# Hedgehog attention beside a gated feed-forward: the last two heads' rows in spare rows of the output projection

## The chip, the cores and the metric

The kernel runs on one core of a Trainium2 chip. The core has five engines that run side by side and wait for each other through semaphores: TensorE (PE in the profile, with PEld for its weight loads), VectorE (DVE), ScalarE (ACT), GpSimd (POOL) and SyncE (SP), which here only issues DMA transfers. Each engine takes its instructions in order. The metric is the time of one execution on the device in microseconds; the kernel before has a median of 693.31 us in three runs (691.02 to 696.13).

## The reference

All tensors are float32. The sequence has S = 2048 tokens, the model width is D = 640, there are H = 32 heads of Dh = 20, and the feed-forward width is F = 1536.

```python
xn = layernorm(x)
q, k, v = split(xn @ wqkv)                       # 32 heads of 20
phi(u) = concat(softmax(u @ w_phi), softmax(-(u @ w_phi)))    # 40 features for each head
kv = sum over tokens of phi(k)^T v               # 40 x 20 for each head
z  = sum over tokens of phi(k)
o  = (phi(q) kv) / (phi(q) z + 1e-6)
s  = o @ wo
g  = silu(gelu(xn @ w1 + b1) @ w2 + b2)
return x + s * g
```

## The kernel before, in words

**Precision.** Nearly all products run in float32r on operands split into a high part and a remainder: three matmuls (PASSES, L296: high x high, high x low, low x high) stand for one float32 product.

**Phase 1** (L436 to L560) works through sixteen token tiles of 128: layer norm, projections, the two softmaxes, and the sum kv over the tokens. The unnormalized query features of each tile go to DRAM (e_dram).

**Feed-forward** (L834 to L960) consists of twelve units: two halves of the tokens (1024 each) by six groups of 256 hidden columns. A unit has seven products of 128x512 blocks (PARTS, a Strassen-like scheme), gelu, and two calls of `down` (L638), which multiply by w2 for the two 512-token chunks of the half and add to the accumulators y. Beside them the units normalize query tiles: `q_norm` (L689) is a generator whose steps are placed by hand between the products. It multiplies the features by the key sums on POOL (L692), sums heads and takes reciprocals on DVE (L694 to L705), scales on POOL (L346) and stores to phi_dram on SP (L709). The table QN (L819) says which tiles a unit takes; units 1 to 5 and 7 to 10 take tiles 8 to 15 and 0 to 3. Unit 11, the last, takes none.

**Output projection** (L984 to L1001) has four chunks of 512 tokens in the order 2, 3, 0, 1. For each chunk `num_groups` (L760) transposes the normalized query features (`num_t`, L729) and multiplies them by the kv of the heads (`num_m`, L742). The 1280 features stand in eleven tiles: ten of 120 rows (three heads of 40) and one of 80 (heads 30 and 31). Two tiles make one output tile oT[0][j], j = 0 to 4: rows 0 to 59 hold three heads of 20, rows 64 to 123 the next three, and eight rows are spare and zero. Heads 30 and 31 have 40 rows, for which there is a tile of their own, oT[1]: they are put three times below each other, by two matmuls of 64 and 56 columns (L753, L754), as high, high and low copies (the selectors lowsel and midsel), so that one matmul of 120 rows does the three passes. `finish` (L800) makes one block of 128 output columns by 512 tokens: 15 matmuls over the five oT tiles and a sixteenth for the last two heads (L803) with the weights `wol` (L711). DVE multiplies the result by the gate, POOL adds the residual, and SP stores it (L815).

The work on a chunk's products is done one chunk ahead. For the first chunk it runs inside the last call of `down` (L959), in groups of three, and the first `finish` follows. For the others it runs between the blocks of the chunk before, in groups of four: block, transposes, and the products of the group before. Query tiles 4 to 7 are normalized during the first two chunks (`late_q`, L964), since their phi is first loaded for the fourth chunk (L998, in the second chunk after its fourth block).

**Order.** From the first unit on every engine's order is that of the program, written by hand (`manual_schedule`, L832); on PE and SP it is so from the start. SP's order therefore matters: it holds the loads of the residual (`load_res`, L780, two blocks ahead of use), the loads and stores of the query tiles, the phi loads (`load_phi`, L723) and the result stores. The buffers come from pools: 23 slabs, 11 rows, and 13 tiles in the pool of the late stage; an instruction that fills a buffer waits until its last user is done.

Of the kernel before, what the change touches and what calls it, by code (L numbers as in the profile page):

```python
# [8 lines left out]
F32 = mybir.dt.float32  # L9
F32R = mybir.dt.float32r  # L10
# [35 lines left out]
def hedgehog_gated_mlp_kernel(ctx: ExitStack, tc: tile.TileContext, x, xt_in, wqk, bd, wv, wo, w1, b1, w2, b2, out_t):  # L46
# [33 lines left out]
    def row(shape, dt, name):  # L80
        return rows.tile(shape, dt, tag="R", name=name)
# [27 lines left out]
    for h in range(3):  # L109
# [4 lines left out]
    lowsel = const.tile([P, 1], F32, name="lowsel")  # L114
    nc.gpsimd.memset(lowsel[:], -1.0)
    nc.gpsimd.affine_select(out=lowsel[:], in_=lowsel[:], pattern=[[0, 1]],
                            compare_op=OP.is_ge, fill=0.0, base=-80, channel_multiplier=1)
    midsel = const.tile([P, 1], F32, name="midsel")
    nc.gpsimd.memset(midsel[:], -1.0)
    nc.gpsimd.affine_select(out=midsel[:], in_=midsel[:], pattern=[[0, 1]],  # L120
                            compare_op=OP.is_ge, fill=0.0, base=-40, channel_multiplier=1)
    nc.gpsimd.affine_select(out=midsel[:], in_=midsel[:], pattern=[[0, 1]],
                            compare_op=OP.is_ge, fill=0.0, base=79, channel_multiplier=-1)
    const.tile([P, 8], F32, name="align")
    bdk = const.tile([P, 10, 64], F32, name="bdk")
    bdl = const.tile([P, 120], F32, name="bdl")


    def load_x(t):
# [442 lines left out]


    def kv_state(kvr):
        nc.gpsimd.memset(bdk[:, :, 60:], 0.0)
        ps = bankB()
        for g, m in enumerate((P, P, 96)):
            nc.tensor.transpose(ps[:120, g * P:g * P + m], kvr[:m, 120 * g:120 * g + 120], ident[:m, :m])
        s3 = ps[:120, :320].rearrange("p (f r) -> p f r", r=32)
        nc.vector.tensor_tensor(bdk[:120, :, :60].rearrange("p f (h d) -> p f h d", d=20),  # L580
                                s3[:, :, None, :20].to_broadcast([120, 10, 3, 20]),
                                mask[:120, None, :, None].to_broadcast([120, 10, 3, 20]), op=OP.mult)
        for r in range(3):
            nc.vector.tensor_tensor(bdl[:80, 40 * r:40 * r + 40].rearrange("p (h d) -> p h d", d=20),
                                    ps[:80, None, 320:340].to_broadcast([80, 2, 20]),
                                    mask[:80, :2, None].to_broadcast([80, 2, 20]), op=OP.mult)
    def kv_norm(kvr):
        zf = slab(F32, "zrep")[:].rearrange("p a b -> p (a b)")
        for e, n in enumerate((360, 360, 320, 240)):
# [90 lines left out]
        nc.sync.dma_start(xd_dram[:, :, 1, at(p)], tt)  # L680


    def q_load(t):
        e = slab(F32, "eq")
        ef = e[:].rearrange("p a b -> p (a b)")
        nc.sync.dma_start(ef, e_dram[t])
        return ef

    def q_norm(t, ef):  # L689
        ez = slab(F32, "ez")  # L690
        zv = ez[:].rearrange("p a b -> p (a b)")
        nc.gpsimd.tensor_tensor(zv, ef, zf, op=OP.mult)  # L692
# [12 lines left out]
        nc.vector.tensor_tensor(r3, r3, den[:, :, None].to_broadcast([P, 32, 2]), op=OP.mult)  # L705
        yield
        scale_heads(ef, rc)
        yield
        nc.sync.dma_start(phi_dram[t], ef)  # L709

    def load_wol():  # L711
        raw = row([P, D], F32, "raw")
        for r in range(3):
            nc.sync.dma_start(raw[40 * r:40 * r + 40, :], wo[640:680, :])
        wol_h = row([P, D], F32R, "wolh")
        wol = row([P, D], F32R, "wol")
        nc.vector.tensor_copy(wol_h[:120, :], raw[:120, :])
        nc.vector.scalar_tensor_tensor(wol[:120, :], wol_h[:120, :].bitcast(F32), midsel[:120, :], raw[:120, :],
                                       op0=OP.mult, op1=OP.add)
        return wol  # L720


    def load_phi(c):  # L723
        tl = [slab(F32R, "phi", (P, 2 * D)) for _ in range(TPC)]
# [17 lines left out]
    def num_m(j, oT, p, n, ph):  # L742
        po = bankB()
        sl = slice(256 * p, 256 * p + 256)
        if j < 5:
            for e in range(2):
                nc.tensor.matmul(po[64 * e:64 * e + 64, :256], bdk[:n, 2 * j + e, :], ph[:n, e * 256:(e + 1) * 256],  # L747
                                 start=True, stop=True)
            o2 = oT[0][j]
            nc.scalar.activation(o2[:, 0, sl], po[:, :256], AF.Copy)  # L750
            nc.vector.tensor_tensor(o2[:, 1, sl], po[:, :256], o2[:, 0, sl].bitcast(F32), op=OP.subtract)
        else:
            for a, b in ((0, 64), (64, 120)):  # L753
                nc.tensor.matmul(po[a:b, :256], bdl[:n, a:b], ph[:n, :256], start=True, stop=True)  # L754
            o2 = oT[1]
            nc.scalar.activation(o2[:120, 0, sl], po[:120, :256], AF.Copy)
            nc.vector.scalar_tensor_tensor(o2[:120, 1, sl], o2[:120, 0, sl].bitcast(F32), lowsel[:120, :],
                                           po[:120, :256], op0=OP.mult, op1=OP.add)

    def num_groups(phi, oT, size=4):  # L760
        steps = [(j, p) for p in range(2) for j in range(6)]
        before = []
        for k in range(0, 12, size):
            now = [(j, p, *num_t(phi, p, j)) for j, p in steps[k:k + size]]
            for j, p, n, ph in before:
                num_m(j, oT, p, n, ph)
            before = now
            yield
        for j, p, n, ph in before:
            num_m(j, oT, p, n, ph)  # L770
        yield

    def new_oT(home):
# [26 lines left out]
    def finish(c, d, oT, last):  # L800
        ps = bankB()
        steps = [(wo_s[j][:, b, d * P:(d + 1) * P], oT[0][j][:, a, :]) for j in range(5) for a, b in PASSES]
        steps.append((wol[:120, d * P:(d + 1) * P], oT[1][:120, 1, :]))  # L803
        for n, (w, o) in enumerate(steps):
            nc.tensor.matmul(ps[:], w, o, start=n == 0, stop=n == 15)  # L805
        xr, gt = xres.pop((c, d)), gates.pop((c, d))
        for o in range(2):
            sl = slice(o * W2, (o + 1) * W2)
            g = gt[:, sl]
            nc.vector.tensor_tensor(g, ps[:, sl], g, op=OP.mult)  # L810
            (nc.vector if last else nc.gpsimd).tensor_tensor(xr[:, sl], g, xr[:, sl], op=OP.add)
            if last:
                nc.sync.dma_start(out_t[d * P:(d + 1) * P, c * CW + o * W2:c * CW + (o + 1) * W2], xr[:, sl])
        if not last:
            nc.sync.dma_start(out_t[d * P:(d + 1) * P, c * CW:(c + 1) * CW], xr[:])  # L815


    zf, none = None, iter(())
    QN = {1: (8,), 2: (9,), 3: (10,), 4: (11,), 5: (12,), 7: (13, 14), 8: (15, 0), 9: (1, 2), 10: (3,)}  # L819
    units = NH * NG  # L820

    def w2_raw(g):
# [11 lines left out]
    for unit in range(units):  # L834
# [116 lines left out]
        if unit == NG - 1:  # L951
            held = list(ys)
            ys[:] = [None] * KC
    wol = load_wol()
    oT = new_oT(late)
    qe[4] = q_load(4)
    load_res(0)
    load_res(1)
    for _ in down(g, w2g, hs, 1, num_groups(phi, oT, 3)):  # L959
# [2 lines left out]
    gate(1)  # L962

    def late_q():  # L964
        qn = q_norm(4, qe.pop(4))
        next(qn)
        for t in range(4, 8):
            if t < 7:
                qe[t + 1] = q_load(t + 1)
            next(qn)  # L970
            yield
            next(qn)
            yield
            next(qn)
            next(qn)
            yield
            next(qn, None)
            if t < 7:
                qn = q_norm(t + 1, qe.pop(t + 1))
                next(qn)  # L980
            yield

    lq = late_q()
    for ci, c in enumerate(ORDER):  # L984
        nxt = iter(())
        if ci + 1 < NCH:
# [2 lines left out]
        for d in range(KC):  # L989
# [4 lines left out]
            if ci == 0 and d % 2 == 0:  # L994
                next(lq, None)
            next(nxt, None)
            if ci + 2 < NCH and d == (0 if ci == 0 else 3):
                phin = load_phi(ORDER[ci + 2])  # L998
            next(lq, None)
# [5 lines left out]
def _layout(A_x, A_wqkv, A_w_phi, A_wo, B_w1, B_b1, B_w2, B_b2):  # L1005
# [5 lines left out]
    wo = np.zeros((680, D), a["wo"].dtype)  # L1011
    for k in range(10):
        wo[64 * k:64 * k + 60] = a["wo"][60 * k:60 * k + 60]
    wo[640:] = a["wo"][600:]
# [37 lines left out]
```

## Time and profile before

| what | value |
|---|---|
| median of three runs | 693.31 us (691.02 to 696.13) |
| span of the profiled execution, first to last instruction | 688.8 us |
| the profiled execution's own time | not recorded beside its span |
| what the median has above that span | 4.5 us |
| mean granted TensorE clock | 0.996 of full speed |
| unit 11 (544.7 to 581.4) | 36.7 us |
| output projection, four chunks (581.4 to 683.95) | 102.6 us |
| from the last matmul to the end | 4.85 us |

A group in the profile is given by its line, engine and operation, then output and inputs by the program's names, shapes, the number of instructions, the busy time in us and the mean of one in ns, and last the engine's idle time ahead of them with what ended it. Matmuls overlap in the pipeline, so the mean of one is longer than the distance from one start to the next. A row of the timeline has start and length in us, engine, line, and how many instructions of a kind were merged; in brackets stands the wait ahead of the first. A row of the windows has, for each engine, the busy time and the number of instructions in that stretch. SPq rows are transfers as SP issues them.

### The profile page before, as it was taken

What the parts mean: (1) busy time and instruction counts of PE and PEld (TensorE: products, weight loads), DVE (VectorE), ACT (ScalarE), POOL (GpSimd) and SP (SyncE); (2) the same over time, 40 slices, a digit from 0 to 9 for tenths busy, and PEclk for the clock granted to TensorE, in tenths of its full rate; (3) what the DMA queues carried; (4) which work ended last, traced back from release to release, by engine and by line L of the source; (5) the groups of instructions that cost most, each with busy time, mean ns of one, the idle gap of its engine ahead of it and who ended that gap; (6) DMA issues with size and microseconds to landing.
All of it is one profiled execution on the core that took longest, in us unless ns stands there. A gap on an engine that the chain in (4) does not pass through costs nothing.

```text
span 688.8 us, 12182 instructions
## 1 busy us (share of the span) xinstructions
PE 680.1 (99%) x4833; PEld 592.8 (86%) x4833; DVE 453.4 (66%) x730; ACT 251.3 (36%) x398; POOL 376.8 (55%) x336
## 2 busy tenths in 40 slices
PE   8899999999999999999999999999999999999997
PEld 8899999999999998888888888888888887777875
DVE  4688556887667546667978774677977655774232
ACT  3331322332332227343353346632232353425430
POOL 1354344948587455946878853636356640783221
PEclk9999999999999999999999999999999999999999
DMA  9830052824172144328697697276364391886633
GB/s 327 288 104 2 3 149 79 245 68 160 35 212 77 72 145 169 115 69 292 220 328 253 202 429 323 81 272 230 140 218 152 132 391 65 320 292 203 234 92 107
DMA packets 73967, 125.57 MB, mean 182 GB/s; under 512 B 5694, under 2 KB 42686, under 8 KB 73014
## 3 DMA queue, kind: packets, MB, share of 16 engines
q1 hardware_dynamic: 71606, 114.31, 48.8%
q10 hardware_dynamic: 2304, 10.49, 4.3%
q8 instruction: 38, 0.62, 0.4%
q14 instruction: 19, 0.16, 0.1%
HBM read 79.68 MB, written 45.10 MB: 181 GB/s over the span
## 4 chain that ended last, share of the span: by engine, by line
PE 96%; DMA 1%; DVE 1%; issue 1%; POOL 1%; ACT 0%; SPq 0%; POOLq 0%; DVEq 0%
PE pA L307 30%; PE pB L646 24%; PE pB L617 21%; PE pB L805 11%; PE pB L747 3%; PE pA L164 2%; PE pB L736 2%; PE kv L378 2%; DMA folds<-in_wqk_dram 1%; PE pA L293 1%; PE pB L754 1%; PE pB L591 0%; POOL e L328 0%; POOL wv L138 0%; ACT e L333 0%
## 5 line engine op out<-in xcount | busy, mean ns | idle before, releaser
L646 PE MATMUL pB<-hs,w2s 128*128 128x512 f32 x720 | 167.1, 390 | 0.0
L646 PEld LDWEIGHTS pB<-hs,w2s 128*128 128x128 f32 x720 | 134.7, 188 | 29.3 <-PE pB L747 0.8
L617 PE MATMUL pB<-xp,w1s 128*128 128x512 f32 x324 | 81.3, 389 | 0.0
L617 PE MATMUL pB<-xd,w1s 128*128 128x512 f32 x324 | 79.3, 389 | 0.0
L333 ACT ACTIVATE e<-e 128x1280 f32<-128x1280 f32 x32 | 40.7, 1271 | 90.0 <-POOL e L328 90.0
L805 PE MATMUL pB<-oT,wo 128*128 128x512 f32 x300 | 72.9, 395 | 0.0
L655 DVE TENSOR_TENSOR y<-pB,y 128x512 f32<-128x512 f32 x100 | 63.8, 680 | 12.3 <-PE pB L646 12.1
L617 PEld LDWEIGHTS pB<-xd,w1s 128*128 128x128 f32 x324 | 60.8, 188 | 12.6
L617 PEld LDWEIGHTS pB<-xp,w1s 128*128 128x128 f32 x324 | 60.8, 188 | 12.6
L805 PEld LDWEIGHTS pB<-oT,wo 128*128 128x128 f32 x300 | 55.4, 188 | 14.8 <-ACT ph L739 1.2
L346 POOL TENSOR_TENSOR e<-e,rc 128x1280 f32<-128x1280 f32 x16 | 39.0, 2438 | 49.1 <-DVE rc L366 48.8
L346 POOL TENSOR_TENSOR eq<-eq,rc 128x1280 f32<-128x1280 f32 x16 | 37.9, 2370 | 50.2 <-DVE rc L705 50.2
L328 POOL TENSOR_TENSOR e<-nr,e 128x640 f32<-128x640 f32 x32 | 45.5, 1422 | 34.6 <-DVE nr L327 31.7
L307 PE MATMUL pA<-wv,xp 128*128 128x320 f32 x384 | 61.1, 312 | 0.8 <-DVE nr L327 0.4
L307 PE MATMUL pA<-wk,xp 128*128 128x320 f32 x384 | 61.5, 316 | 0.0
L622 ACT ACTIVATE pB<-pB,b1t 128x512 f32<-128x512 f32 x48 | 31.8, 662 | 76.2 <-PE pB L617 26.7
L307 PE MATMUL pA<-wq,xp 128*128 128x320 f32 x384 | 59.0, 309 | 0.0
L307 PEld LDWEIGHTS pA<-wk,xp 128*128 128x128 f32 x384 | 58.3, 193 | 0.2
L307 PEld LDWEIGHTS pA<-wv,xp 128*128 128x128 f32 x384 | 56.9, 188 | 1.7 <-issue 0.7
L307 PEld LDWEIGHTS pA<-wq,xp 128*128 128x128 f32 x384 | 56.9, 188 | 0.1
L692 POOL TENSOR_TENSOR ez<-eq,zrep 128x1280 f32<-128x1280 f32 x16 | 47.3, 2958 | 0.5 <-DMA eq<-e_dram 0.5
L402 POOL TENSOR_TENSOR w1s<-raw,w1s 128x640 fp32r<-128x640 f32 (+1 forms) x18 | 25.7, 1429 | 37.1 <-ACT w1s L401 29.9
(139 smaller groups left out, 1045.2 us busy)
## 6 DMA issues: line engine op xcount, KB each, us to landing
raw<-in_w_dram SPq DMA_DIRECT2D x42, 320.0 KB, 4.4
e_dram<-e ACTq DMA_DIRECT2D x16, 640.0 KB, 4.0
eq<-e_dram SPq DMA_DIRECT2D x16, 640.0 KB, 7.0
phi_dram<-eq SPq DMA_DIRECT2D x16, 640.0 KB, 3.5
phi<-phi_dram SPq DMA_DIRECT2D x16, 640.0 KB, 8.5
xt<-in_x_dram SPq DMA_DIRECT2D x16, 320.0 KB, 4.9
xres<-in_xt_dram SPq DMA_DIRECT2D x20, 256.0 KB, 4.8
out_dram<-xres SPq DMA_DIRECT2D x18, 256.0 KB, 3.0
```

The source lines that it names most:

```text
L307: nc.tensor.matmul(ps[:, hf, :HALF], stat_x(q, o, k, a), ws[k][:, b, hf * HALF:(hf + 1) * HALF], start=n == 0, stop=n == 3 * KC - 1)
L328: nc.gpsimd.tensor_tensor(e5[:, :, :, 1, :], nr[:, :, :, None].to_broadcast([P, 2, 16, DH]), e5[:, :, :, 0, :], op=OP.subtract)
L333: nc.scalar.activation(ef, ef, AF.Exp)
L346: nc.gpsimd.tensor_tensor(e3, e3, rc[:, :, None].to_broadcast([P, 64, DH]), op=OP.mult)
L402: nc.gpsimd.tensor_tensor(sl[:, 1, :n], src, sl[:, 0, :n].bitcast(F32), op=OP.subtract)
L617: nc.tensor.matmul(bank[ch][:], tl[:, a, off + wo_:off + wo_ + P], mov(blk, b), start=new and n == 0, stop=n == len(mms) - 1, skip_group_c ...
L622: nc.scalar.activation(ps, ps, AF.Gelu_apprx_tanh, bias=b1t[:, f:f + 1])
L646: nc.tensor.matmul(ps[:], ws[i][:, b, d * P:(d + 1) * P], hs[o][i][:, a, :], start=i == n == 0, stop=(i, n) == (GF - 1, 2), skip_group_che ...
L655: nc.vector.tensor_tensor(y, ps[:], y, op=OP.add)
L692: nc.gpsimd.tensor_tensor(zv, ef, zf, op=OP.mult)
L747: nc.tensor.matmul(po[64 * e:64 * e + 64, :256], bdk[:n, 2 * j + e, :], ph[:n, e * 256:(e + 1) * 256], start=True, stop=True)
L805: nc.tensor.matmul(ps[:], w, o, start=n == 0, stop=n == 15)
```

## The change

Heads 30 and 31 lose their own sixteenth matmul. Their 40 output rows are shared out to the 40 spare rows of the five oT[0][j] tiles, eight to each. For this the layout of an oT tile changes: every sixteenth row (15, 31, ... 127) is spare, and the rows between hold five-row pieces of three heads; the rows of wo are permuted in the same way on the host (640 rows in place of 680). kv_state builds the block weights bdk in that order, by three multiplications in place of one, and bdl once in place of three times. `num_m` computes the last two heads with one matmul of 40 columns. A new function `spread(j, oT)` copies eight rows of oT[1], high and low part (8 x 4 KB), into the spare rows of oT[0][j], by a transfer from SBUF to SBUF on SP's queue, right after the second half (p = 1) of tile j is done. The products start with j = 5, so that their rows are there first. `load_wol`, lowsel and midsel go.

In the output projection the result stores, and the phi stores of `late_q`, are collected (`put`) and issued by `put_all` after the step of `num_groups` in the same block, and so behind the spread transfers on SP. Query tile 4 moves from `late_q` to unit 11 (QN); its load moves to unit 10, its store is issued in unit 11 on SP, and `late_q` begins with tile 5.

```diff
     def kv_state(kvr):
-        nc.gpsimd.memset(bdk[:, :, 60:], 0.0)
+        nc.gpsimd.memset(bdk[:, :, 15::16], 0.0)
...
-        nc.vector.tensor_tensor(bdk[:120, :, :60].rearrange("p f (h d) -> p f h d", d=20),
-                                s3[:, :, None, :20].to_broadcast([120, 10, 3, 20]),
-                                mask[:120, None, :, None].to_broadcast([120, 10, 3, 20]), op=OP.mult)
-        for r in range(3):
-            nc.vector.tensor_tensor(bdl[:80, 40 * r:40 * r + 40].rearrange("p (h d) -> p h d", d=20),
-                                    ps[:80, None, 320:340].to_broadcast([80, 2, 20]),
-                                    mask[:80, :2, None].to_broadcast([80, 2, 20]), op=OP.mult)
+        for h in range(3):
+            nc.vector.tensor_scalar(
+                bdk[:120].rearrange("p f (q c) -> p f q c", c=16)[:, :, :, 5 * h:5 * h + 5],
+                s3[:, :, :20].rearrange("p f (q i) -> p f q i", i=5), mask[:120, h:h + 1], None, op0=OP.mult)
+        nc.vector.tensor_tensor(bdl[:80].rearrange("p (h d) -> p h d", d=20),
+                                ps[:80, None, 320:340].to_broadcast([80, 2, 20]),
+                                mask[:80, :2, None].to_broadcast([80, 2, 20]), op=OP.mult)
...
+    stores, late_store = [], [False]
+
+    def put(dst, src):
+        if late_store[0]:
+            stores.append((dst, src))
+        else:
+            nc.sync.dma_start(dst, src)
+
+    def put_all():
+        while stores:
+            nc.sync.dma_start(*stores.pop(0))
...
-        nc.sync.dma_start(phi_dram[t], ef)
+        put(phi_dram[t], ef)
...
-            for a, b in ((0, 64), (64, 120)):
-                nc.tensor.matmul(po[a:b, :256], bdl[:n, a:b], ph[:n, :256], start=True, stop=True)
+            nc.tensor.matmul(po[:40, :256], bdl[:n, :], ph[:n, :256], start=True, stop=True)
             o2 = oT[1]
-            nc.scalar.activation(o2[:120, 0, sl], po[:120, :256], AF.Copy)
-            nc.vector.scalar_tensor_tensor(o2[:120, 1, sl], o2[:120, 0, sl].bitcast(F32), lowsel[:120, :],
-                                           po[:120, :256], op0=OP.mult, op1=OP.add)
+            nc.scalar.activation(o2[:40, 0, sl], po[:40, :256], AF.Copy)
+            nc.vector.tensor_tensor(o2[:40, 1, sl], po[:40, :256], o2[:40, 0, sl].bitcast(F32), op=OP.subtract)
+
+    def spread(j, oT):
+        nc.sync.dma_start(oT[0][j][15::16].bitcast(F32), oT[1][8 * j:8 * j + 8].bitcast(F32))
 
     def num_groups(phi, oT, size=4):
-        steps = [(j, p) for p in range(2) for j in range(6)]
+        steps = [(j, p) for p in range(2) for j in (5, 0, 1, 2, 3, 4)]
         before = []
+
+        def products(group):
+            for j, p, n, ph in group:
+                num_m(j, oT, p, n, ph)
+                if p and j < 5:
+                    spread(j, oT)
...
-        steps.append((wol[:120, d * P:(d + 1) * P], oT[1][:120, 1, :]))
         for n, (w, o) in enumerate(steps):
-            nc.tensor.matmul(ps[:], w, o, start=n == 0, stop=n == 15)
+            nc.tensor.matmul(ps[:], w, o, start=n == 0, stop=n == 14)
...
         if not last:
-            nc.sync.dma_start(out_t[d * P:(d + 1) * P, c * CW:(c + 1) * CW], xr[:])
+            put(out_t[d * P:(d + 1) * P, c * CW:(c + 1) * CW], xr[:])
...
-    QN = {1: (8,), 2: (9,), 3: (10,), 4: (11,), 5: (12,), 7: (13, 14), 8: (15, 0), 9: (1, 2), 10: (3,)}
+    QN = {1: (8,), 2: (9,), 3: (10,), 4: (11,), 5: (12,), 7: (13, 14), 8: (15, 0), 9: (1, 2), 10: (3,), 11: (4,)}
...
-    wol = load_wol()
     oT = new_oT(late)
-    qe[4] = q_load(4)
+    qe[5] = q_load(5)
...
     lq = late_q()
+    late_store[0] = True
...
             next(nxt, None)
+            put_all()
             if ci + 2 < NCH and d == (0 if ci == 0 else 3):
                 phin = load_phi(ORDER[ci + 2])
```

More of the change, by code (lines that the diff above doesn't have):

```diff
@@ L113, in hedgehog_gated_mlp_kernel @@
                                 compare_op=OP.is_ge, fill=0.0, base=40 * h + 39, channel_multiplier=-1)
[L114 to L123, printed above, removed]
     const.tile([P, 8], F32, name="align")
     bdk = const.tile([P, 10, 64], F32, name="bdk")
-    bdl = const.tile([P, 120], F32, name="bdl")
+    bdl = const.tile([P, 40], F32, name="bdl")
     def load_x(t):
@@ L708, in q_norm @@
         yield
-        nc.sync.dma_start(phi_dram[t], ef)
[L711 to L720, printed above, removed]
+        put(phi_dram[t], ef)
     def load_phi(c):
@@ L752, in num_m @@
         else:
-            for a, b in ((0, 64), (64, 120)):
-                nc.tensor.matmul(po[a:b, :256], bdl[:n, a:b], ph[:n, :256], start=True, stop=True)
+            nc.tensor.matmul(po[:40, :256], bdl[:n, :], ph[:n, :256], start=True, stop=True)
             o2 = oT[1]
-            nc.scalar.activation(o2[:120, 0, sl], po[:120, :256], AF.Copy)
-            nc.vector.scalar_tensor_tensor(o2[:120, 1, sl], o2[:120, 0, sl].bitcast(F32), lowsel[:120, :],
-                                           po[:120, :256], op0=OP.mult, op1=OP.add)
+            nc.scalar.activation(o2[:40, 0, sl], po[:40, :256], AF.Copy)
+            nc.vector.tensor_tensor(o2[:40, 1, sl], po[:40, :256], o2[:40, 0, sl].bitcast(F32), op=OP.subtract)
+    def spread(j, oT):
+        nc.sync.dma_start(oT[0][j][15::16].bitcast(F32), oT[1][8 * j:8 * j + 8].bitcast(F32))
     def num_groups(phi, oT, size=4):
-        steps = [(j, p) for p in range(2) for j in range(6)]
+        steps = [(j, p) for p in range(2) for j in (5, 0, 1, 2, 3, 4)]
         before = []
+        def products(group):
[3 more added lines that the diff above has]
+                    spread(j, oT)
         for k in range(0, 12, size):
             now = [(j, p, *num_t(phi, p, j)) for j, p in steps[k:k + size]]
-            for j, p, n, ph in before:
-                num_m(j, oT, p, n, ph)
+            products(before)
             before = now
             yield
-        for j, p, n, ph in before:
-            num_m(j, oT, p, n, ph)
+        products(before)
         yield
@@ L964, in late_q @@
     def late_q():
-        qn = q_norm(4, qe.pop(4))
+        qn = q_norm(5, qe.pop(5))
         next(qn)
-        for t in range(4, 8):
+        for t in range(5, 8):
             if t < 7:
@@ L1010, in _layout @@
     bd = np.zeros((P, 6, 64), a["wphi"].dtype)
[L1011 to L1014, printed above, removed]
+    wo = np.zeros((D, D), a["wo"].dtype)
+    w4 = wo.reshape(10, 4, 16, D)
+    w4[:, :, :15] = a["wo"][:600].reshape(10, 3, 4, 5, D).transpose(0, 2, 1, 3, 4).reshape(10, 4, 15, D)
+    w4[:, :, 15] = a["wo"][600:].reshape(10, 4, D)
     for h in range(H):
```

## The prediction

> **What bounds the kernel now.** I read the page from the top: the busy shares, then the chain that ended last, then the tail of the run by stretches, since the change sits there.
>
> ```profile
> span 688.8 us, 12182 instructions
> PE 680.1 (99%) x4833; PEld 592.8 (86%) x4833; DVE 453.4 (66%) x730; ACT 251.3 (36%) x398; POOL 376.8 (55%) x336
> PE 96%; DMA 1%; DVE 1%; issue 1%; POOL 1%; ACT 0%; SPq 0%; POOLq 0%; DVEq 0%
> PE pA L307 30%; PE pB L646 24%; PE pB L617 21%; PE pB L805 11%; PE pB L747 3%; PE pA L164 2%; PE pB L736 2%; PE kv L378 2%; DMA folds<-in_wqk_dram 1%; PE pA L293 1%; PE pB L754 1%; PE pB L591 0%; POOL e L328 0%; POOL wv L138 0%; ACT e L333 0%
> ```
>
> TensorE is the chain, 96% of it, and the lines that the change edits (L805, L754) are on it. The same by stretches: the last feed-forward unit, then the four chunks of the output projection.
>
> ```profile
> 544.69:581.39 36.70, 36.70 (x210) 28.53 (x209) 19.89 (x34) 18.44 (x38) 9.85 (x7) 1.00 0.74 272
> 581.39:609.36 27.97, 27.97 (x173) 21.65 (x172) 19.43 (x38) 9.70 (x24) 18.86 (x13) 1.00 0.75 271
> 637.36:665.52 28.16, 28.16 (x174) 21.66 (x172) 8.43 (x22) 13.90 (x31) 7.13 (x10) 1.00 0.51 179
> 665.52:683.95 18.43, 18.43 (x81) 14.86 (x79) 4.64 (x12) 0.00 (x0) 5.72 (x8) 1.00 0.38 115
> ```
>
> The columns are length, then PE, PEld, DVE, ACT, POOL, clock, DMA share. PE fills each stretch; the others have room (DVE 19.4 of 28.0, POOL 9.9 of 36.7). So a matmul taken out is worth its spacing, and something added counts only where PE has to wait for it.
>
> **The change part by part.**
>
> *The sixteenth matmul of each output block goes (L803).* The mean of one matmul in a group is latency, since matmuls overlap; the price is the distance to the next start.
>
> ```profile
> L805 PE MATMUL pB<-oTl,wol 120*128 120x512 f32 x20 | 7.9, 395 | 0.0
> 584.79 0.40 PE L805 MATMUL pB<-oTl,wol 120*128 120x512 f32 x1
> 585.03 1.41 PE L736 MATMUL pB<-identr,phi 128*120 128x128 f32 x16
> 609.13 0.40 PE L805 MATMUL pB<-oTl,wol 120*128 120x512 f32 x1
> 609.36 3.58 PE L805 MATMUL pB<-oT,wo 128*128 128x512 f32 x15
> ```
>
> 584.79 to 585.03 and 609.13 to 609.36 are 0.23 to 0.24 us, not 0.395. Twenty of them: 20 x 0.23 = 4.6 us.
>
> *The product of the last two heads loses one of its two matmuls (L753).* Each f32 matmul leaves two records, so four records become two, at eight places.
>
> ```profile
> 591.18 1.95 PE L747 MATMUL pB<-ph,bdk 120*64 120x256 f32 x16
> 593.06 3.69 PE L805 MATMUL pB<-oT,wo 128*128 128x512 f32 x15
> L754 PE MATMUL pB<-ph,bdl 80*64 80x256 f32 x16 | 4.8, 379 | 0.0
> L754 PE MATMUL pB<-ph,bdl 80*56 80x256 f32 x16 | 4.8, 379 | 0.0
> ```
>
> Sixteen records of the same 256 columns take 593.06 - 591.18 = 1.88 us, 0.118 us each. The sixteen that go are worth 16 x 0.118 = 1.9 us. Together PE loses 6.5 us, the ceiling of what removed work alone can give.
>
> *Twenty transfers (spread) are added on SP's queue.* Each moves 8 rows of 4 KB, five per chunk. Two prices: the landing, which the next output block waits for, and SP's time and order, since SP waits in order for the eviction that a transfer copies, with loads queued behind.
>
> First the landing. The trace has no such transfer; these are its neighbours on the same queue (KB each, median us to landing).
>
> ```profile
> out_dram<-xres SPq DMA_DIRECT2D x4, 128.0 KB, 1.9
> st_dram<-pst SPq DMA_DIRECT2D x4, 2.0 KB, 3.1
> xres<-in_xt_dram SPq DMA_DIRECT2D x20, 256.0 KB, 4.8
> eq<-e_dram SPq DMA_DIRECT2D x16, 640.0 KB, 7.0
> phi<-phi_dram SPq DMA_DIRECT2D x16, 640.0 KB, 8.5
> ```
>
> For 32 KB I take 3.0, near the 2 KB row, with 1.9 and 8.5 as ends. The tightest place is the first chunk, where the last group of products stands six matmuls ahead of the block that reads them.
>
> ```profile
> 578.46 1.08 PE L747 MATMUL pB<-ph,bdk 120*64 120x256 f32 x8
> 579.57 0.86 DVE L751 TENSOR_TENSOR oT<-pB,oT 128x256 fp32r<-128x256 f32 x2 [0.32 <-ACT oT L750]
> 580.44 0.48 DVE L757 SCALAR_TENSOR_TENSOR oTl<-oTl,lowsel,pB 120x256 fp32r<-120x256 f32 x1
> 581.39 3.56 PE L805 MATMUL pB<-oT,wo 128*128 128x512 f32 x15
> ```
>
> By the new order this group is j = 2, 3, 4; its evictions end as here, at about 580.0, 580.45 and 580.9, and the transfers leave then. The block starts at 581.39 and reads j = 2 after six matmuls of 0.227 (3.56 for fifteen, less the last one's latency), at 582.75; j = 4 at 584.1. So j = 2 has 2.7 us and j = 4 has 3.2. A landing of 3.0 costs 0.3 us here. I take 0.6, since loads moved by the next part may still drain ahead; ends 0 (landing 1.9) and 2.1 (landing 4.8). In the later chunks a whole block lies between: in the rows below (T is the end of the block, 631.62), j = 1 is evicted at T + 1.6 and read after 1.9 of products, a block of 15 x 0.227 = 3.4 and three matmuls, at T + 6.1. It has 4.5 us, so a landing of 3.0 is hidden.
>
> The Trainium skill, "DMA: Bandwidth & Descriptors", Anatomy of one DMA, fits a fixed 2.0 us and the bytes over 436 GB/s (on the GpSimd path); for 32 KB an estimate of 2.1 us. By that no read waits and the sum would be 0.6 us better, 688.2; our small transfers, 1.9 and 3.1, stand on both sides of it.
>
> Now the order on SP. In the second chunk the loads of the fourth chunk's phi tiles follow the fourth block's store.
>
> ```profile
> 631.39 0.39 PE L805 MATMUL pB<-oTl,wol 120*128 120x512 f32 x1
> 631.71 1.52 PE L747 MATMUL pB<-ph,bdk 120*64 120x256 f32 x12
> 632.83 1.29 DVE L751 TENSOR_TENSOR oT<-pB,oT 128x256 fp32r<-128x256 f32 x3 [0.25 <-ACT oT L750]
> 633.77 0.34 SPq L815 DMA_DIRECT2D out_dram<-xres  x1
> 634.13 0.48 DVE L757 SCALAR_TENSOR_TENSOR oTl<-oTl,lowsel,pB 120x256 fp32r<-120x256 f32 x1
> 634.16 2.11 SPq L726 DMA_DIRECT2D phi<-phi_dram  x4
> 641.01 1.55 PE L736 MATMUL pB<-identr,phi 128*120 128x128 f32 x16
> 641.14 1.28 PEld L736 LDWEIGHTS pB<-identr,phi 128*120 128x120 f32 x15 [0.22 <-DMA phi<-phi_dram]
> ```
>
> The loads leave at 634.16, and PE already waits 0.22 us for them at 641: they have no slack. In the new kernel SP first issues four transfers, the last after the fourth eviction (634.61), then the store (0.34), then the loads: 634.65 + 0.4 + 0.4 = 635.45, 1.3 us later. PE meanwhile comes two matmuls, 0.46 us, earlier. The wait grows by 1.3 + 0.46 less what rounding leaves: 1.6 us. This is paid once; the first chunk's phi loads come after its first block, without spreads beside them. Ends: 0, if the first two tiles land quicker, and 2.5.
>
> *Query tile 4 moves into the last unit.* DVE gets two reductions and five small operations, POOL two multiplications; SP a load one unit earlier and a store.
>
> ```profile
> L692 POOL TENSOR_TENSOR ez<-eq,zrep 128x1280 f32<-128x1280 f32 x16 | 47.3, 2958 | 0.5 <-DMA eq<-e_dram 0.5
> L346 POOL TENSOR_TENSOR eq<-eq,rc 128x1280 f32<-128x1280 f32 x16 | 37.9, 2370 | 50.2 <-DVE rc L705 50.2
> 543.53 3.10 POOL L138 TENSOR_TENSOR w2s<-raw,w2s 128x640 fp32r<-128x640 f32 x2
> 557.61 6.96 PE L646 MATMUL pB<-hs,w2s 128*128 128x512 f32 x30
> 561.15 7.91 POOL L138 TENSOR_TENSOR wo<-raw,wo 128x640 fp32r<-128x640 f32 x5 [14.53 <-ACT wo L136]
> 585.23 0.75 DVE L810 TENSOR_TENSOR gt<-pB,gt 128x256 f32<-128x256 f32 x2 [2.95 <-PE pB L805]
> ```
>
> POOL's 2.96 us pushes the w2 split from 546.6 to 549.6; PE needs it at 557.61, so it is covered. The 2.37 us scaling stands behind the wo splits, which end at 569.06, so the store leaves SP at about 571.4. Behind it wait the load of tile 5 and the four loads for blocks 0 and 1, 2.3 MB with the store. At the 272 GB/s of the first window row that is 8.5 us, until about 580; DVE first needs them at 585.23. Covered, with 5 us left; without the cover each us goes to the first evictions, not at once to PE. The two slabs held longer delay loads for the second chunk that are first read at 585.03. I take 0.
>
> *The rest.* load_wol goes: one load wait and two DVE operations in the first chunk, and three of eleven row buffers. It can return part of the small PE waits between 557.6 and 581.4; I take -0.2, ends -1.0 and 0: 23.8 us less 60 matmuls of 0.227, 48 f32 records of 0.118 and 44 transposes of 0.08 (row 585.03, without the last one's latency) leaves about 1.0 of waits. The residual loads now wait on SP behind the transfers and the stores put off behind these: each is issued two blocks ahead, 2 x 3.6 us, against a delay of 1 to 2 us: 0. The order of the heads in a group changes, not the number of products: 0. The multiplications of kv_state, three in place of one and one in place of three, run on DVE in unit 6 and are first read in unit 11: 0. Five POOL instructions at the start go, but the chain there waits for the folds loads: 0.
>
> **Sum:** -4.6 - 1.9 + 0.6 + 1.6 - 0.2 = -4.5 us. The span of 688.8 becomes 684.3. The profiled execution shows only its span; the median of the runs, 693.31, is 4.5 above it, and I keep that: 693.3 - 4.5 = **688.8 us**.
>
> **The rivals.** *All is hidden.* The phi loads come in time, no transfer is waited for, and the first chunk's small waits go: -6.5 - 1.0 = -7.5, 685.8 us. For it: DMA share is 0.51 to 0.75 in the chunks, so there is room. Against: the 0.22 us wait above shows that the phi loads already come last.
>
> *The transfers land late* (the other side). With a landing of L, the first chunk waits L - 2.7 and each of three others L - 4.5, and the phi loads cost 1.6. The loss equals the 6.7 of gain at 4L - 14.6 = 6.7, L = 5.3 us. At 7.0 (the eq row) the loss is 13.4: 693.3 + 6.7 = 700.0 us; at 8.5 it is 706.0. For it: the two large rows. Against: they move twenty times the bytes.
> The Trainium skill's same page, HWDGE ordering, says a semaphore increment lands only after every earlier write of that DMA engine; by that a transfer behind a 640 KB load or store lands with it. No row here shows a small transfer behind a large one.
>
> *The gain stays in the product groups.* PE's time per block falls, but where products follow (12 of 20 blocks), PE would wait as much longer for their evictions. Then only 8 x 0.23 is gained, and 2.2 - 0.2 lost: 693.4 us. Against: no other engine is full in the windows.
>
> **How the numbers follow.** The forecast has 0.60, all hidden 0.20, late landing 0.13, gain lost 0.07. A measurement of this kernel tells about 1%, 6.9 us, from no change. Over that only the all-hidden case gives, with a little of the forecast's edge: faster 0.22. Slower by over 1% takes L of 7 or more: 0.08. Within: 0.70. The forecast's own ends are -6.5 and about -1.7; the range takes in the all-hidden case below and the lost gain above: 685.3 to 693.5.
>
> **What would show it.** Twenty matmuls of 120x512 gone and sixteen records at the 80-row product; chunks of about 26.4 us instead of 28.0, the last of 17.3; the third chunk with a wait of nearly 2 us of PE's weight load on phi; the first block with a wait of under 1 us on an oT transfer; spreads landing in 2 to 3 us. Wrong, if spreads take over 5 us, if PE waits for them in later chunks, or if the last unit grows beyond 36.7 us.

## The result, and the profile after

The changed kernel takes 699.12 us against 695.72 us for the kernel before (medians of 22 runs each); the ratio is 1.0057, 95% interval 1.0034 to 1.0080. One run of the changed kernel, 703.94 us, counts as a slow one and is left out of the ratio. The ratio makes it 4.0 us slower (2.4 to 5.6; the medians differ by 3.4), where 4.5 us less was forecast. The 699.1 lies above the range of 685.3 to 693.5; moved up by the 2.4 us that the 22 runs put on the base of 693.31, the range would end at 695.9, still below it.

The head of the page after, to be held against the rows shown before:

```profile
span 700.1 us, 12153 instructions
PE 685.0 (98%) x4797; PEld 596.6 (85%) x4797; DVE 453.6 (65%) x728; ACT 251.5 (36%) x398; POOL 375.7 (54%) x331
PE 87%; DVE 6%; DMA 3%; issue 1%; POOL 1%; ACT 1%; SPq 1%; DVEq 0%; POOLq 0%
```

PE has 36 matmul records less, but its share of the chain falls from 96 to 87%: DVE has 6% and DMA 3% of it now, where each had 1%. This execution also began about 5 us later with its last unit, for a reason that is not the change (last section), so I compare from the start of that unit. These are windows of the kernel after: the last unit, then the four chunks, each from its first output matmul to the next chunk's.

```profile
550.50:591.25 40.75, 37.77 (x203) 28.95 (x202) 24.89 (x38) 18.94 (x38) 14.19 (x9) 0.96 0.63 236
591.25:617.93 26.68, 26.68 (x164) 20.72 (x163) 18.79 (x38) 9.63 (x24) 18.37 (x13) 1.00 0.83 286
617.93:645.18 27.25, 27.10 (x165) 20.76 (x164) 10.77 (x27) 12.85 (x28) 10.13 (x12) 1.00 0.60 195
645.18:678.02 32.84, 29.40 (x165) 22.54 (x164) 8.30 (x22) 13.93 (x31) 7.09 (x10) 0.90 0.54 166
678.02:695.29 17.27, 17.27 (x77) 13.97 (x75) 4.63 (x12) 0.00 (x0) 5.72 (x8) 1.00 0.48 151
```

And the kernel before: the last unit from the same point (the window in the prediction began three matmuls earlier), and the second chunk, the one that the prediction does not show:

```profile
545.37:581.39 36.02, 36.02 (x207) 27.97 (x206) 19.67 (x33) 18.44 (x38) 9.17 (x6) 1.00 0.73 269
609.36:637.36 28.00, 28.00 (x174) 21.68 (x172) 14.98 (x34) 12.92 (x28) 14.91 (x14) 1.00 0.76 232
```

| stretch, us | before | after | difference |
|---|---|---|---|
| last unit | 36.02 | 40.75 | +4.73 |
| first chunk | 27.97 | 26.68 | -1.29 |
| second chunk | 28.00 | 27.25 | -0.75 |
| third chunk | 28.16 | 32.84 | +4.68 |
| fourth chunk | 18.43 | 17.27 | -1.16 |
| sum | 138.58 | 144.79 | +6.2 |

The first and the fourth chunk became shorter by 1.3 and 1.2 us, the second by 0.75. The forecast had 1.6 for the first three (28.0 to 26.4) and 1.1 for the fourth. Two places pay more than that back. In both PE is idle for about 3 us (PE busy 37.77 of 40.75, 29.40 of 32.84) and in both the granted clock falls (0.96 and 0.90).

**The last unit.** The timeline after, where tile 4's steps stand:

```profile
566.28 7.64 POOL L128 TENSOR_TENSOR wo<-raw,wo 128x640 fp32r<-128x640 f32 x5 [11.60 <-ACT wo L126]
569.45 1.55 DVE L702 TENSOR_TENSOR dn<-dn,rc 128x64 f32<-128x64 f32 x1
571.04 1.44 DVE L705 SCALAR_TENSOR_TENSOR den<-dn 128x32 f32<-128x32 f32 x1
572.51 0.35 DVE L706 RECIPROCAL den<-den 128x32 f32<-128x32 f32 x1
572.90 1.10 DVE L708 TENSOR_TENSOR rc<-rc,den 128x64 f32<-128x64 f32 x1
573.92 1.28 DVE L646 TENSOR_TENSOR y<-pB,y 128x512 f32<-128x512 f32 x2
574.65 0.52 PE L727 MATMUL pB<-identr,phi 128*120 128x128 f32 x4 [2.82 <-DVE y L646]
```

Operations on 128x64 and 128x32 elements take 1.1 to 1.55 us while POOL splits wo; the reciprocal between them takes 0.35, as in all its sixteen calls. Behind them DVE's additions of y come late, and PE, which needs the banks that these free, waits 2.82 us.

**The third chunk.** SP and PE after, from the fourth block of the second chunk (block end and products at 639.88):

```profile
639.88 1.95 PE L738 MATMUL pB<-ph,bdk 120*64 120x256 f32 x16
641.46 2.56 SPq L750 DMA_DIRECT2D oT<-oTl  x4
644.11 0.40 SPq L684 DMA_DIRECT2D out_dram<-xres  x1
644.56 2.08 SPq L717 DMA_DIRECT2D phi<-phi_dram  x4
651.11 0.30 PE L727 MATMUL pB<-identr,phi 128*80 128x128 f32 x1 [2.26 <-DMA phi<-phi_dram]
652.59 1.77 PE L727 MATMUL pB<-identr,phi 128*80 128x128 f32 x13 [1.18 <-DMA phi<-phi_dram]
654.16 5.33 PE L801 MATMUL pB<-oT,wo 128*128 128x512 f32 x15
```

The phi loads leave 4.7 us after the products begin, against 2.45 before (634.16 less 631.71). PE waits 2.26 + 1.18 us, and then a block of 15 matmuls takes 5.33 us instead of 3.7.

### The profile page after: what moved, and what is told of

Its sections match the earlier page's. It is cut to its first block, busy times and chain, and to the rows that moved or that the text cites. A ratio compares the mean times of both kernels' runs of the same rounds, so it can differ in the third digit from the quotient of the medians.

```text
span 700.1 us, 12153 instructions
## 1 busy us (share of the span) xinstructions
PE 685.0 (98%) x4797; PEld 596.6 (85%) x4797; DVE 453.6 (65%) x728; ACT 251.5 (36%) x398; POOL 375.7 (54%) x331
## 4 chain that ended last, share of the span: by engine, by line
PE 87%; DVE 6%; DMA 3%; issue 1%; POOL 1%; ACT 1%; SPq 1%; DVEq 0%; POOLq 0%
PE pA L297 30%; PE pB L637 21%; PE pB L608 19%; PE pB L801 8%; PE pA L154 3%; PE pB L738 2%; PE kv L368 2%; PE pB L727 2%; DVE y L646 1%; DMA eq<-e_dram 1%; DMA phi<-phi_dram 1%; DMA folds<-in_wqk_dram 1%; PE pA L283 1%; DVE dn L331 1%; PE pB L744 0%
```

## The experiments

Theory A: the two idle times, each made longer by the clock that falls after it, eat the gain. Theory B: the transfers themselves cost. Theory C: the removed matmuls give nothing, since another engine bounds the chunks. For each kernel I give the ratio to the kernel before with its interval, and the lengths of the last unit and the four chunks, taken from PE's timeline as in the table.

### Tile 4 back where it was (e1_tile4_late)

```diff
-... 10: (3,), 11: (4,)}
+... 10: (3,)}
-    qe[5] = q_load(5)
+    qe[4] = q_load(4)
...
-        qn = q_norm(5, qe.pop(5))
+        qn = q_norm(4, qe.pop(4))
...
-        for t in range(5, 8):
+        for t in range(4, 8):
```

> The changed kernel with query tile 4 put back into the late steps (load, sums, scaling and store as before the change). Theory A (two waits of TensorE eat the gain: tile 4's VectorE steps in the last unit, slowed while GpSimd splits wo, and the phi loads that stand behind the spread transfers on SP; each wait costs more than its length because the granted clock falls after it): the last unit falls from 40.75 us to about 36.3, the wait on phi at the third chunk stays near 3.4 us, and the time is about 4.5 us below the changed kernel, so about the time before. Theory B (the spread transfers themselves cost, by landing late and holding SP): no more than 1 us below the changed kernel, with waits on oT. Theory C (another engine bounds the chunks, so removed matmuls give nothing): no change in the chunks, and no gain here.

1.0103 (1.0067 to 1.0138): 35.94, 26.70, 31.04, 32.79, 17.27. The last unit falls as theory A said, but the second chunk grows by 3.8 us. Theory A did not have that; theory B had waits on oT, and a gain of at most 1 us:

```profile
606.26 0.42 SPq L689 DMA_DIRECT2D eq<-e_dram  x1
607.09 2.56 SPq L750 DMA_DIRECT2D oT<-oTl  x4
612.46 4.38 PE L801 MATMUL pB<-oT,wo 128*128 128x512 f32 x12 [2.59 <-DMA oT<-oTl]
```

The transfers leave 0.8 us after a 640 KB load, and PE gets the first of the four 5.4 us after it left. In the changed kernel the last such load leaves 8.7 us before the transfers (607.38 and 616.06), and PE goes on 3.0 us after the first of the four leaves, with a wait of 0.15. So tile 4's move does something for the transfers: it takes the load out of the queue just ahead of them.

### Phi loads ahead of the transfers (e2_phi_first)

```diff
             load_res(ci * KC + d + 2)
+            if ci == 1 and d == 3:
+                phin = load_phi(ORDER[3])
...
-            if ci + 2 < NCH and d == (0 if ci == 0 else 3):
+            if ci == 0 and d == 0:
                 phin = load_phi(ORDER[ci + 2])
```

> The changed kernel with the fourth chunk's phi loads issued at the head of the fourth block of the second chunk, ahead of the four spread transfers and of the stores put off. Theory A: TensorE's wait on phi at the third chunk (3.4 us) goes, the clock stays at 1.00 there, that chunk falls from 32.75 to about 26.4 us, and the time is about 6 us below the changed kernel. Theory B: the spread transfers now stand behind 2.6 MB of loads and land late, TensorE waits on oT at the third chunk by 2 us or more, and less than half of the 6 us is gained. Theory C: the chunk stays above 28 us.

1.0106 (1.0079 to 1.0134): 39.14, 26.69, 27.25, 34.96, 17.27. The wait on phi is gone and a longer one on oT has taken its place:

```profile
635.98 2.13 SPq L717 DMA_DIRECT2D phi<-phi_dram  x4
638.37 3.56 SPq L750 DMA_DIRECT2D oT<-oTl  x4
648.57 5.36 PE L801 MATMUL pB<-oT,wo 128*128 128x512 f32 x12 [5.52 <-DMA oT<-oTl]
```

The first of the transfers left at 638.37, behind 2.6 MB, and PE can go on 10.2 us later. This is what theory B expected here, and the rival "the transfers land late", not in the changed kernel but in this one. The rule of the Trainium skill that the prediction names, "DMA: Bandwidth & Descriptors", HWDGE ordering (a completion lands only after the earlier writes of its DMA engine), agrees with the two rows on transfers, here and in e1_tile4_late. That the rule is the cause is not shown: a queue that works off its bytes in turn would look the same. Theory A was too narrow: as the loads are placed here, one of the two, phi or the transfers, has to wait for the other on this queue.

### Both (e3_both)

> Both edits: tile 4 late as before the change, and the phi loads ahead of the spread transfers. What is left of the change is the removed matmuls and the spread transfers. Theory A: 6.5 us below the kernel before (ratio about 0.991), the last unit about 36.3 us, the chunks 27.0, 26.4, 26.5 and 17.3. Theory B: no better than 3 us below before, with waits on oT. Theory C: within 1 us of before.

1.0092 (1.0063 to 1.0121): 35.94, 26.69, 32.90, 34.80, 17.27. It is 6.4 us slower than before where theory A had 6.5 us less, and both waits on oT are there (4.22 and 5.91 us in its timeline), as theory B had it. Theory C is not the reason, since the first and the fourth chunk keep their gain.

### Tile 4's steps early in the last unit (e5_tile4_early)

```diff
         p3 = part(w1g, bank, 3)
+        if not more:
+            next(q1, None)
...
+        if not more:
+            next(q1, None)
         c21 = part(w1g, bank, 5)
...
         if not more:
+            next(q1, None)
+            next(q1, None)
             phin = load_phi(ORDER[1])
```

> The changed kernel with tile 4 still in the last unit, but its VectorE steps and its scaling put between the unit's seven products, ahead of the split of wo on GpSimd. The work of VectorE and GpSimd is the same, only beside other work. Theory A (lock: the small VectorE operations with two SBUF inputs took 1.1 to 1.55 us beside a GpSimd operation and 0.2 us alone): they take 0.2 us each, TensorE's wait on the y additions goes, the unit falls to about 36.3 us and the time is 4.5 us below the changed kernel. Rival A2 (plain load: VectorE has simply more to do in the unit): the unit keeps most of its 4 us. Theory B: no change.

1.0019 (0.9998 to 1.0039): 35.94, 26.70, 27.07, 31.97, 17.27. The last unit is as short as before the change (36.02). By the ratios the kernel is 2.6 us faster than the changed one, where 4.5 was expected. The same work in another place costs nothing:

```profile
561.42 0.22 DVE L702 TENSOR_TENSOR dn<-dn,rc 128x64 f32<-128x64 f32 x1
561.68 0.19 DVE L705 SCALAR_TENSOR_TENSOR den<-dn 128x32 f32<-128x32 f32 x1
561.90 0.35 DVE L706 RECIPROCAL den<-den 128x32 f32<-128x32 f32 x1
562.29 0.23 DVE L708 TENSOR_TENSOR rc<-rc,den 128x64 f32<-128x64 f32 x1
568.24 7.67 POOL L128 TENSOR_TENSOR wo<-raw,wo 128x640 fp32r<-128x640 f32 x5 [3.21 <-DMA phi_dram<-eq]
```

POOL has nothing to do between 556.64 and 562.66, so no POOL operation runs beside the four. The steps also stand elsewhere here, but the rows give the share of the slowing: from the first of the four to the end of the last are 4.55 us in the changed kernel and 1.10 here, and the difference, 3.45 us, is more than the 2.82 and 0.17 us that PE waited. So it was not DVE's load (rival A2) but the POOL operation beside it. The Trainium skill, "SBUF — State Buffer", Who interferes with whom, says that a DVE operation with two SBUF inputs and a GpSimd operation that reads SBUF exclude each other for a whole instruction. The rows fit: the three that took 1.1 to 1.55 us have two SBUF inputs, the reciprocal has one. That the port is the cause is the page's account; the runs show only that it hangs on what POOL does.

### Tile 4 early, and the phi loads two blocks earlier (e6_queue_clear)

```diff
-            if ci + 2 < NCH and d == (0 if ci == 0 else 3):
+            if ci + 2 < NCH and d == ci:
```

> The changed kernel with tile 4's steps early in the last unit (as in e5_tile4_early) and the fourth chunk's phi loads issued two blocks earlier, after the second block of the second chunk, so that 2.6 MB have landed before the last spread transfers leave. Theory D (a transfer lands only behind all that was issued before it on the queue, so what matters is how much stands ahead when it leaves): no wait on phi, no wait on oT, clock 1.00 throughout; from the start of the last unit to the last matmul about 132 us against 138.6 before; ratio about 0.991. Theory B (the transfers cost by themselves): waits on oT of 1 us or more stay in some chunk. Theory C: within 1 us of before.

0.9936 (0.9912 to 0.9959), 691.06 us against 695.58: 35.94, 26.70, 27.05, 26.80, 17.27, in all 133.76 against 138.58. It is faster than the kernel before, and by the ratios than the changed one. Now the four transfers leave 12.4 us after the loads, and PE waits for neither:

```profile
624.14 1.98 SPq L717 DMA_DIRECT2D phi<-phi_dram  x4
636.50 2.57 SPq L750 DMA_DIRECT2D oT<-oTl  x4
643.74 1.24 PE L727 MATMUL pB<-identr,phi 128*80 128x128 f32 x14
644.82 3.69 PE L801 MATMUL pB<-oT,wo 128*128 128x512 f32 x15
```

All that theory D expected of the waits and of the clock (1.00 in all five windows) is there; B, by which a wait of 1 us or more stays, and C fall. The gain is 4.8 us in the trace, not the 6.5 that I had put on the removed work; the kernel without the sixteenth matmul, below, says why.

### Filling the wait (e4_fill_wait)

```diff
+            if ci == 2 and d == 0:
+                pd = bankB()
+                for n in range(14):
+                    nc.tensor.matmul(pd[:], wo_s[0][:, 0, :P], oT[0][0][:, 0, :], start=n == 0, stop=n == 13)
             next(nxt, None)
```

> The changed kernel with 14 matmuls of 128x512 whose product is not used (3.2 us), placed on TensorE where it waits for phi at the third chunk. They bring nothing forward. Theory K (the wait costs twice, since the granted clock falls after it): the block after the wait takes 3.7 us in place of 5.3, the third chunk falls from 32.75 to about 30 us, and the time is 2 to 3 us below the changed kernel. Rival (the slow stretch after the wait has another cause, such as the loads): the chunk keeps its 32.75 us, or grows.

1.0038 (1.0011 to 1.0065), against 1.0057 for the changed kernel; the intervals overlap, so only the trace tells: 40.65, 26.69, 27.23, 30.08, 17.27. The third chunk falls by 2.8 us. The second phi tile is there 7.4 us after the loads leave instead of 8.0, which is little of it:

```profile
648.50 3.34 PE L995 MATMUL pB<-oT,wo 128*128 128x512 f32 x14
651.68 1.34 PE L727 MATMUL pB<-identr,phi 128*80 128x128 f32 x14
652.86 3.67 PE L801 MATMUL pB<-oT,wo 128*128 128x512 f32 x15
```

With PE busy the block after the wait takes 3.67 us again, and the granted clock is 1.00 in the whole chunk. The gain fits the slow matmuls of the changed kernel: there PE is busy for 29.40 us in this chunk, against 26.80 in e6_queue_clear. The changed kernel's windows show the granted clock (the third number from the end) after its idle time:

```profile
652.60:656.00 3.40, 3.40 (x18) 3.01 (x19) 0.00 (x0) 2.56 (x5) 0.00 (x0) 0.50 0.97 336
```

The Trainium skill, "TensorE: Matmul & The Clock Gate", Part 1, has this as a gate that halves the clock after an idle window of about 3.4 us and opens after as much busy time; 0.50 agrees. The window does not, and the measurement decides: in e1_tile4_late a wait of 2.59 us without any PE instruction in it was followed by a granted clock of 0.65 over 4.2 us. Nor does a wait always cost the same. The last unit has the same wait of 2.8 us in five kernels, and its granted clock and length were 1.00 and 39.14 us in e2_phi_first, 0.96 and 40.65 to 40.75 in the changed kernel, e4_fill_wait and e12_phi_early, and 0.92 and 41.52 in e11_no_spread.

### Tile 4 alone, in the kernel before (e8_tile4_alone)

The edit is the first one's, the other way round, in the kernel before.

> The kernel before with only query tile 4 moved into the last unit, as the change does. Theory A: the last unit grows from 36.7 to about 41 us, with a wait of TensorE on the y additions of nearly 3 us; 4 us slower than before (ratio 1.006). Rival (the move is harmless, and the wait comes with the new layout or the transfers): within 1 us of before.

1.0144 (1.0111 to 1.0176): 47.74, 27.96, 28.00, 28.00, 18.43. The move alone costs 11.7 us in the old layout, more than twice what I expected. The 2.64 us wait on the y additions is there, and a second, longer one:

```profile
574.95 0.32 SPq L709 DMA_DIRECT2D phi_dram<-eq  x1
575.32 2.59 SPq L714 DMA_DIRECT2D raw<-in_wo_dram  x3
580.85 0.49 DVE L717 CAST wolh<-raw 120x640 fp32r<-120x640 f32 x1 [7.23 <-DMA raw<-in_wo_dram]
582.73 1.98 PE L747 MATMUL pB<-ph,bdk 120*64 120x256 f32 x8 [5.62 <-DVE oT L751]
```

Tile 4's store waits on SP for POOL's scaling, load_wol's loads wait behind it, DVE waits for them, and PE for DVE. In the changed kernel load_wol is gone, so only the first wait is left.

### The sixteenth matmul alone (e10_matmul_alone)

This is the kernel before; its output lacks the last two heads.

```diff
-        steps.append((wol[:120, d * P:(d + 1) * P], oT[1][:120, 1, :]))
...
-            nc.tensor.matmul(ps[:], w, o, start=n == 0, stop=n == 15)
+            nc.tensor.matmul(ps[:], w, o, start=n == 0, stop=n == 14)
```

> The kernel before without the sixteenth matmul of each output block; the last two heads are left out of the output. It prices that removal by itself. Theory of the spacing: 20 x 0.23 = 4.6 us less from the start of the output projection to the last matmul, 98.0 us against 102.6, less what the phi loads at the third chunk take back (they already came last): up to 0.5 us and the clock after it. Theory C: under 2 us less.

0.9934 (0.9908 to 0.9959): 36.00, 26.75, 26.88, 27.84, 17.29. The chunks lose 3.8 us, and with the 0.72 us that PE now waits for phi it is 4.5: the spacing was the right price.

```profile
645.03 1.42 PE L736 MATMUL pB<-identr,phi 128*120 128x128 f32 x15 [0.72 <-DMA phi<-phi_dram]
```

It is as fast as e6_queue_clear, which in addition does one matmul less for the last two heads, eight times. That saving, my second term of 1.9 us, is not to be seen. The reason is in the timeline of the changed kernel:

```profile
599.26 1.22 PE L727 MATMUL pB<-identr,phi 128*120 128x128 f32 x14
600.41 0.41 PE L744 MATMUL pB<-ph,bdl 80*40 80x256 f32 x1
600.42 0.43 PE L738 MATMUL pB<-ph,bdk 120*64 120x256 f32 x1
600.66 0.38 PE L744 MATMUL pB<-ph,bdl 80*40 80x256 f32 x1
600.69 1.64 PE L738 MATMUL pB<-ph,bdk 120*64 120x256 f32 x11
602.26 3.70 PE L801 MATMUL pB<-oT,wo 128*128 128x512 f32 x15
```

These 14 records take 602.26 - 600.41 = 1.85 us, the sixteen before 1.88. The first two of them start 0.01 us apart. Before, all sixteen do so two by two, in eight steps of 0.21 to 0.27 us; after, the fourteen still need eight such steps, and the last two records stand alone. So half of a pair taken away saves nothing.

### No transfers (e11_no_spread)

This is the changed kernel; its output lacks the last two heads.

```diff
-                if p and j < 5:
-                    spread(j, oT)
```

> The changed kernel without the twenty transfers; the last two heads are left out of the output. Theory E (the transfers hold SP: four of them take 2.56 us of it ahead of the phi loads): the phi loads leave about 2.5 us earlier after the fourth block, the wait on phi at the third chunk falls from 3.4 us to about 0.8, as in e10_matmul_alone, the clock does not fall there, and the third chunk is about 27 us. Rival (the wait comes from the store put off, or from the matmuls taken away): more than 2 us of wait stay.

One run, 696.84 us: 41.52, 26.70, 26.80, 27.16, 17.27. The phi loads leave 2.5 us after the products begin, and the wait is gone:

```profile
640.47 1.95 PE L738 MATMUL pB<-ph,bdk 120*64 120x256 f32 x16
642.98 2.12 SPq L717 DMA_DIRECT2D phi<-phi_dram  x4
649.28 1.59 PE L727 MATMUL pB<-identr,phi 128*80 128x128 f32 x14
```

So it was the transfers' time on SP that made phi late, not the store put off.

### Phi loads earlier, tile 4 as changed (e12_phi_early)

> The changed kernel with the phi loads after the second block of the second chunk, as in e6_queue_clear, but tile 4's steps left as changed. If the two costs add up: no wait on phi and none on oT at the third chunk, the last unit still 40.7 us; 5.5 to 6.5 us below the changed kernel, so about 1 to 2 us below before (ratio 0.997 to 0.999). Rival (one cost hides the other): as fast as e6_queue_clear, or no gain.

0.9997 (0.9968 to 1.0027): 40.73, 26.69, 27.26, 26.80, 17.27. In the traces the two costs add up: 6.0 us for phi, 4.8 us for tile 4. The runs give less: by the ratios the kernel is 4.2 us below the changed one, where 5.5 to 6.5 were expected.

### Each transfer twice (e13_double_spread)

This is e6_queue_clear with one more edit:

```diff
-        nc.sync.dma_start(oT[0][j][15::16].bitcast(F32), oT[1][8 * j:8 * j + 8].bitcast(F32))
+        for _ in range(2):
+            nc.sync.dma_start(oT[0][j][15::16].bitcast(F32), oT[1][8 * j:8 * j + 8].bitcast(F32))
```

> As e6_queue_clear, but each transfer is issued twice, with the same contents. Theory D (with a short queue transfers cost TensorE nothing): PE waits less than 1 us more in all, though SP issues another 20 x 0.6 us; within 1 us of e6_queue_clear. Theory B (transfers cost by themselves): 2 us or more above it.

1.0574 (1.0522 to 1.0627): 39 us slower than before, where about the time of e6_queue_clear was expected. My reading of the edit was wrong: the second transfer writes the rows that the first writes, so SP waits until the first has landed. SP's waits:

```profile
SPq L751 <- DMA oT<-oTl: 35.3, 20, 3.0
```

This measures the landing instead, 35.3/20 = 1.8 us after 0.57 us of issue, about 2.3 us with little ahead. It tells nothing for or against theory B.

### The control (e14_before_phi_early)

> The kernel before with only the phi loads moved to after the second block of the second chunk. The control for e6_queue_clear: the wait in the kernel before was 0.22 us, so the gain is under 0.5 us (ratio 0.999 to 1.000). If instead it gains 2 us or more, e6_queue_clear owes part of its gain to this and not to the removed matmuls.

0.9988 (0.9959 to 1.0018): 36.00, 27.97, 28.00, 28.00, 18.43. Early phi loads give the kernel before only the 0.2 us that it waited, so e6_queue_clear owes its gain to the removed matmuls.

## Why the prediction was wrong, point by point

- *Sixteenth matmul, 4.6 us:* right (4.5 us).
- *Half of the last two heads' product, 1.9 us:* wrong. I divided 1.88 us by sixteen records; they come in pairs that run together, and the saving is 0.2 us at most (8 x 0.03).
- *Landing of the transfers, 3.0 us, 0.6 us of cost:* near. About 2.3 us with little ahead; the first chunk shows no wait, the second one of 0.15 us. The rival of late landing did not come true in the changed kernel; waits of its kind came only in e1_tile4_late, e2_phi_first and e3_both, which have a load just ahead.
- *Phi loads, 1.6 us:* right in mechanism, mis-sized. The delay was 2.2 us and not 1.3, since the four transfers hold SP for 2.56 us in a row, 0.57 us or more each; the prediction let them keep step with the evictions and counted 0.4 for the last. The wait was 3.4 us; why the second tile landed 8 us after the loads left, and not 6.98 as before, stays open. The larger error is that I counted a wait at its length: with 2.6 us of slow matmuls after it, it cost 6.0 us (32.84 against 26.80).
- *Tile 4: "I take 0".* This step failed outright. I covered POOL's work, SP's store and its loads, and did not cost DVE's steps where they stand. It cost 4.8 us in this trace (40.75 against 35.94): 3.0 us of idle PE and 1.8 us of slow matmuls. Where the clock stayed up, in e2_phi_first, it cost 3.2. The trace of the kernel before had the sign in the smallest, the middle and the largest time in ns, where the mean, 444, hides that there are two kinds:

```profile
L699 DVE TENSOR_TENSOR dn<-dn,rc x16: 215/225/1176, 307.8 to 619.5; 128x64 f32<-128x64 f32 x16
```

- *The rest, -0.2 us:* near. With nothing to wait for, the last unit is 35.94 us (e6_queue_clear) against 36.02.
- *Sum:* -4.7 for the matmuls (e6_queue_clear shows -4.8 with both waits gone), +4.8, +6.0 and +0.2 make +6.3; the table has +6.2. The 22 runs give +4.0 (2.4 to 5.6). The table is one execution, and that the clock does not always fall after the same wait, as e2_phi_first shows, can be part of the difference; how much is not shown.

## What to carry to other kernels

Cost every step that is moved beside the operations that will stand next to it, and look at the smallest and largest time of an instruction, not its mean. A small transfer may land as late as what stands ahead of it on its queue (about 2.3 us with little ahead, 5.4 behind one load, 10.2 behind four), so space the large loads around it and count its issue time for what comes behind. On a chain that is full of matmuls an idle time can cost more than its length: here about 3 us cost 3.2 to 5.6, and 3.4 cost 6.0.

## What the runs showed of the hardware that I had not expected

How fast the matmuls run at the start differs from execution to execution and is no property of the kernel: the mean granted clock of the first 20 us was 0.71 to 1.00 in the profiles, and the last unit began at 544.2 us where it was 1.00 (e3_both), at 552.5 where it was 0.71 (e5_tile4_early). Before and after, this is 545.4 at 0.91 and 550.5 at 0.73. The old layout has late starts too: e10_matmul_alone began its last unit at 550.9 with 0.75. The time lost fits: in the next 20 us the clock was 1.00 before and 0.93 after, which makes 20 x (0.09 + 0.00) = 1.8 us lost before and 20 x (0.27 + 0.07) = 6.8 after, 5.0 of the 5.1 us between them. So spans of single profiles differ by up to 8 us at the start alone.

A transfer of 8 rows of 4 KB takes 0.57 us of SP's time, where a store of 128 rows took 0.34.
